# Linear attention and a softplus MLP on one core: small attention products in pairs, and an instruction planner that counts TensorE's changes of shape

## The chip, the core and the metric

The kernel runs on one core of one Trainium2 chip. The metric is the device time of the whole kernel in microseconds (us); lower is better. Times of runs are medians. The profile is one execution with the hardware profiler on; its span is close to the timed runs but not equal to them.

## What is computed

Attention without softmax, an RMS norm per head, and then an MLP with softplus:

```python
kv  = einsum('bhsd,bhse->bhde', k, v)        # batch 8, heads 8, seq 576, head_dim 64
o   = einsum('bhsd,bhde->bhse', q, kv)
x   = o / sqrt(mean(o*o, -1) + 1e-6) * g_norm
x   = x.transpose(0, 2, 1, 3).reshape(4608, 512)
out = softplus(x @ w_in) @ w_out             # w_in 512 x 2048, w_out 2048 x 512
```

All inputs are float32 in range and accuracy, and the result has to keep float32 accuracy.

## The kernel before, in words

**Exact products from three.** The large matmuls use TensorE's fp32r type. To keep float32 accuracy every operand is split into three parts (`high`, `low`, `less`, on ACT and DVE), and every product is three matmuls that are summed in PSUM.

**Attention.** For each batch `kv_of` (L625) forms k times v in five pieces of eight 64-wide matmuls (four pieces of 512 positions, one of the remaining 64), summed in one PSUM bank; the matmuls are at L654. The k and v tiles of the four main pieces come from the ring `e`, which has four slots, two for each piece; those of the fifth have slots of their own. For each of the 36 tiles of 128 tokens, `rows` (L660) turns q, multiplies it with kv in sixteen 64x64 matmuls (`out_rows`, L673), and normalizes: square on ACT, sum on DVE, the root on GpSimd, the product on DVE. The first twelve tiles are turned by TensorE (L691 for x, L729 for q); later ones are turned on DVE and go through HBM. These small products use only a part of TensorE's array at a time, unlike all other matmuls, which use all 128x128 of it. In the trace each of these float32 matmuls has two records, so that a piece of L654 is x16 and a tile of L673 is x32.

**MLP, first pass.** `step` (L798) takes a block of 384 tokens and one chunk of 128 of the 2048 hidden units: twelve matmuls of 384 columns (L812), softplus and splitting, then three groups of three matmuls of 512 columns (L819), one for each 128 tokens, summed in PSUM over the chunks of the block. Four blocks take 4 chunks and eight take 6: 64 steps. The attention work of later tokens is mixed in between.

**MLP, wide passes.** `wide_step` (L977) takes 512 tokens and a pair of chunks, with seven products (a fast scheme in the manner of Strassen) instead of eight, each of six matmuls of 256 columns (L999), with copies and sums on ACT and DVE in between (L1040, L1044, L1023, L1026, L1048), then splitting (L1056, L1059, L1062) and eight groups of three matmuls of 512 columns (L1069). There are 48 such steps in two passes. Their inputs, sums and differences of parts of x, are prepared by `units_of` (L892): loads of x and of forms that were kept (L909), a subtraction on DVE (L923), and the split (L959 on ACT, L962 and L965 on DVE). Weights of later chunks are converted from their raw form (L393 to L423), stored, loaded again (L508), combined (`both`, L512) and split. At the end of a group of steps `leave` (L857) copies the sums out of PSUM on ACT (L860) and stores them: with a plain store, or in the first wide pass with an accumulating DMA that GpSimd issues (L876). In the second wide pass partial sums are loaded and put into PSUM before (`enter`, L850, loads at L854).

**What sets the order.** No instruction is placed by hand. Every piece of work is a `Task` with an engine, a planned duration, its predecessors, the buffer slots that it takes and gives back, and a position `pos` (`add`, L76). `Plan.order` (L85) simulates the engines: for each engine it finds the tasks that could start first, looks at all that could start within `SOON` = 150 ns after that, and takes the one of lowest `pos`. The order that comes out is the order in which the instructions are issued; each engine then runs its own in that order, waiting for semaphores. Positions come from the 79 numbers in `P0` to `P3` (L232 to L236): when weights are fetched and converted, how early x and k, v and q are prepared, how the groups of a wide step lie against each other. Where TensorE would have nothing to do in the plan before the first pass is under way, the planner puts in a warm-up matmul (`warm`, L1148, recorded at L1150).

Of the kernel before, what the change touches and what calls it, by code (L numbers as in the profile page):

```python
# [55 lines left out]
class Plan:  # L56
# [18 lines left out]

    def add(self, engine, ns, run, after=(), pos=0.0, take=(), give=(), size=0, behind=None, follows=None):  # L76
# [5 lines left out]
        t.behind = behind  # L82
        return t

    def order(self):  # L85
# [30 lines left out]
        dma_free = 1500  # L116
        last_read = {}
        done, left = [], len(self.tasks)
        while left:
            best = None  # L120
            for engine, tasks in ready.items():
                options = []
                for t in tasks:
                    at = max(engine_free[engine], t.ready)
                    if t.size:
                        at = max(at, dma_free - 2500)
                    for i, s in enumerate(t.take):
                        others = sum(u.ring == s.ring for u in t.take[:i])
                        if engine == "SP" and s.ring in ("m", "n"):
                            others += self.KEEP  # L130
                        if len(free[s.ring]) <= others:
                            break
                        at = max(at, sorted(free[s.ring])[sum(u.ring == s.ring for u in t.take[:i])][0])
                    else:
                        options.append((at, t))
                if not options:
                    continue
                first = min(at for at, _ in options)
                at, t = min(((at, t) for at, t in options if at <= first + self.SOON),
                            key=lambda o: (o[1].pos, o[0]))  # L140
                if engine == "PE" and self.spare and self.spare[-1].start is None:
                    ring, run, ns, _ = self.spare
                    begin = max(engine_free["PE"], self.BEGIN, min(free[ring])[0] if free[ring] else at)
                    if begin + ns <= at:
                        s = Slot(ring)
                        at, t = begin, Task("PE", ns, lambda s=s: run(s), [], None, [s], [s], 0)
                        s.readers = 1
                if best is None or at < best[0]:
                    best = (at, t)
# [6 lines left out]
            for s in t.take:  # L156
# [27 lines left out]
def kernel(  # L184
# [24 lines left out]
    nc = tc.nc  # L209
# [21 lines left out]

    P0 = [-56.63, -20.32, -32.46, -13.58, -22.9, -4.89, -7.19, 1.72, -73.06, -41.99, -41.77, -22.79, -44.57, -21.25, -14.8, -8.6, 1.67, -29.08, 17.25, 10.29, 6.58, 8.78, -6.26, 3.54, 1.45, 13.48, -15.35, 7.9, 12.17, 8.99]  # L232
    CONVERT, FETCH, EARLY, LATER = P0[:8], P0[8:16], P0[16:27], P0[27:]
    P1 = [50.69, 53.68, 57.04, 32.49, 105.47, 132.19, 42.4, 60.71, 74.8, 108.41, 128.47, 137.43]
    P2 = [23.63, 36.5, 43.45, 50.53, 60.37, 65.43, 64.44, 117.03, 68.8, 102.64, 29.3, 15.31, 28.43, 80.7, 97.59, 71.63, 81.78, 77.98, 144.53, 143.71, 1.95]
    P3 = [3.31, 1.4, 5.36, -0.89, 1.94, 3.54, 1.55, 2.86, 2.68, -0.6, 3.76, -0.15, 0.77, -1.77, 1.87, 1.35]  # L236
    SPLIT = {p: (P1[i], P1[6 + i]) for i, p in enumerate((2, 3, 4, 5, 6, 7))}
# [379 lines left out]
    kv_ready = {}  # L617
    o_tasks = {}

    def x_pos(t):  # L620
# [4 lines left out]
    def kv_of(b):  # L625
# [4 lines left out]
        bank = slot(f"s{b}" if b < 2 else "tp")  # L630
        last = None
        MAIN = 4 * P
        for p in range(NP + 1):
# [223 lines left out]
    def leave(ph, t, bank, done, pos):  # L857
# [328 lines left out]
```

## Time and profile before

890.5 us median of 3 runs (889.25 to 891.43). The profiled execution spans 893.1 us.

| engine | busy us | share of the span |
|---|---|---|
| PE (TensorE matmul) | 870.3 | 97% |
| PEld (TensorE weight load) | 760.9 | 85% |
| DVE (VectorE) | 684.4 | 77% |
| ACT (ScalarE) | 542.6 | 61% |
| POOL (GpSimd) | 113.9 | 13% |

| group | matmuls (records) | mean ns of one record |
|---|---|---|
| L812, first pass, first product | 768 | 339 |
| L819, first pass, second product | 576 | 398 |
| L999, wide passes, first products | 2016 | 281 to 286 |
| L1069, wide passes, second product | 1152 | 393 to 396 |
| L673, q times kv | 576 (1152) | 223 |
| L654, k times v | 320 (640) | 228 to 233 |

How to read it: the durations of matmuls in the table overlap each other, because TensorE is pipelined, and their ends are modelled. What one more matmul costs is seen from start to start, in the chain of waits or the timeline. DMA moved 157.62 MB in the span, 176 GB/s on the mean.

### The profile page before, as it was taken

The numbers are of one execution on the slowest core, as the hardware profiler recorded it, in microseconds if no ns is written. First come the engines' busy times: TensorE is split into PE (matmuls) and PEld (weight loads), VectorE is DVE, ScalarE is ACT, GpSimd is POOL, SyncE is SP. The second block draws the span as 40 slices with busy tenths as digits, with TensorE's granted clock in tenths as the row PEclk, the third lists the DMA queues.
The fourth block names the chain that finished last, engine by engine and source line by source line (L and its number), as shares of the span: only waits on it lengthen the run. The fifth ranks groups of instructions, "written<-read, shape, count | busy, mean of one in ns | idle before, by whom it ended". The sixth has DMA issues, their size and how long they took to land.

```text
span 893.1 us, 16939 instructions
## 1 busy us (share of the span) xinstructions
PE 870.3 (97%) x6459; PEld 760.9 (85%) x6459; DVE 684.4 (77%) x956; ACT 542.6 (61%) x1015; POOL 113.9 (13%) x115
## 2 busy tenths in 40 slices
PE   7889999999999999999999989999999999999997
PEld 5678888888888899988888978888887988999996
DVE  6888878778688888799998778778776765667662
ACT  4776555435344466776757646556768755666764
POOL 0433321222222200001101101101101000000000
PEclk9999999999999999999999999999999999999999
DMA  9999998589883673548776648657655623566643
GB/s 252 256 239 248 244 208 240 107 183 221 221 168 123 164 226 118 181 138 208 212 201 137 162 128 240 147 153 175 141 153 106 201 90 113 177 188 182 185 130 94
DMA packets 234448, 157.62 MB, mean 176 GB/s; under 512 B 105728, under 2 KB 197888, under 8 KB 234368
## 3 DMA queue, kind: packets, MB, share of 16 engines
q1 hardware_dynamic: 229024, 147.11, 60.7%
q0 software_dynamic: 5184, 9.44, 7.4%
q8 instruction: 50, 0.82, 0.4%
q14 instruction: 30, 0.25, 0.1%
q10 hardware_dynamic: 160, 0.00, 0.0%
HBM read 103.55 MB, written 52.95 MB: 175 GB/s over the span
## 4 chain that ended last, share of the span: by engine, by line
PE 61%; issue 27%; DMA 4%; POOL 3%; DVE 3%; ACT 1%; SPq 0%; POOLq 0%; ACTq 0%; DVEq 0%
PE banks L819 15%; PE banks L812 15%; PE banks L1069 13%; PE banks L999 12%; POOL part L876 3%; PE banks L654 2%; PE banks L673 2%; DMA raw<-in_moe_w_in_dram 1%; DMA part<-m 1%; DMA loads<-in_v_dram 1%; DMA w<-in_q_dram 1%; PE banks L691 1%; DVE g_False L1062 0%; DVE gv L1059 0%; ACT m L860 0%
## 5 line engine op out<-in xcount | busy, mean ns | idle before, releaser
L1069 PE MATMUL banks<-pieces,gv 128*128 128x512 f32 x624 | 195.4, 394 | 0.2 <-ACT m L860 0.2
L812 PE MATMUL banks<-units,pieces 128*128 128x384 f32 x768 | 147.1, 339 | 0.0
L819 PE MATMUL banks<-pieces,gv 128*128 128x512 f32 x576 | 146.5, 398 | 0.0
L999 PE MATMUL banks<-units,pieces 128*128 128x256 f32 x1008 | 140.3, 282 | 0.0
L999 PEld LDWEIGHTS banks<-units,pieces 128*128 128x128 f32 x1008 | 133.6, 190 | 7.5 <-ACT g_True L1023 0.6
L812 PEld LDWEIGHTS banks<-units,pieces 128*128 128x128 f32 x768 | 134.2, 188 | 5.2 <-ACT half L834 0.3
L819 PEld LDWEIGHTS banks<-pieces,gv 128*128 128x128 f32 x576 | 105.7, 188 | 21.2
L1069 PE MATMUL banks<-pieces,g_False 128*128 128x512 f32 x312 | 122.6, 393 | 0.5 <-DVE g_False L1062 0.5
L1069 PEld LDWEIGHTS banks<-pieces,gv 128*128 128x128 f32 x624 | 108.5, 189 | 16.3 <-ACT m L860 0.4
L1059 DVE TENSOR_TENSOR gv<-g_True,gv 128x1024 fp32r<-128x1024 f32 x48 | 58.7, 1223 | 41.7 <-ACT gv L1056 41.4
L834 ACT ACTIVATE half<-banks 128x384 f32<-128x384 f32 x64 | 31.4, 490 | 86.4 <-PE banks L812 85.4
L876 POOL DMA_DIRECT2D part<-m x36 | 31.8, 960 | 329.3 <-ACT m L860 313.9
L1069 PEld LDWEIGHTS banks<-pieces,g_False 128*128 128x128 f32 x312 | 58.6, 188 | 14.8 <-DVE g_False L1062 1.5
L1026 ACT ACTIVATE g_True<-banks 128x256 f32<-128x256 f32 x96 | 36.7, 382 | 52.0 <-PE banks L999 51.1
L681 POOL TENSOR_TENSOR r<-r,half 128x8 f32<-128x8 f32 x36 | 65.8, 1827 | 3.0
L999 PE MATMUL banks<-early,pieces 128*128 128x256 f32 x432 | 61.8, 286 | 4.4 <-ACT banks L1044 3.6
L999 PEld LDWEIGHTS banks<-early,pieces 128*128 128x128 f32 x432 | 58.0, 193 | 8.3 <-ACT banks L1044 5.0
L1062 DVE SCALAR_TENSOR_TENSOR g_False<-gv 128x1024 fp32r<-128x1024 f32 x48 | 58.8, 1225 | 1.5
L962 DVE TENSOR_TENSOR units<-loads,units 128x1024 fp32r<-128x1024 f32 x39 | 47.6, 1221 | 15.3 <-ACT units L959 13.5
L1048 DVE TENSOR_TENSOR g_True<-banks,g_True 128x512 f32<-128x512 f32 x48 | 33.1, 689 | 33.6 <-ACT g_True L1023 20.2
L823 DVE TENSOR_TENSOR gv<-half,gv 128x384 fp32r<-128x384 f32 x64 | 35.3, 552 | 29.4 <-ACT gv L836 28.8
L860 ACT ACTIVATE m<-banks 128x512 f32<-128x512 f32 x72 | 41.8, 595 | 18.0 <-PE banks L1069 10.8
(117 smaller groups left out, 1408.1 us busy)
## 6 DMA issues: line engine op xcount, KB each, us to landing
loads<-x SPq DMA_DIRECT2D x180, 128.0 KB, 2.7
loads<-form SPq DMA_DIRECT2D x45, 256.0 KB, 3.0
part<-m SPq DMA_DIRECT2D x36, 256.0 KB, 3.1
form<-loads SPq DMA_DIRECT2D x36, 256.0 KB, 3.1
part<-m POOLq DMA_DIRECT2D x36, 256.0 KB, 5.6
m<-part SPq DMA_DIRECT2D x36, 256.0 KB, 3.1
raw<-in_moe_w_in_dram SPq DMA_DIRECT2D x16, 512.0 KB, 5.2
loads<-in_k_dram SPq DMA_DIRECT2D x32, 256.0 KB, 4.9
```

What stands on the lines that cost most here:

```text
L681: nc.gpsimd.tensor_tensor(out=r.tile, in0=r.tile, in1=half, op=ALU.pow)
L812: nc.tensor.matmul(hp, lhsT=w_in.tile[:, i, kd * P:(kd + 1) * P], rhs=xv.tile[:, i, kd], start=(m == 0), stop=(m == 3 * KD - 1))
L819: nc.tensor.matmul(mine[i].tile, lhsT=gv.tile[:, m, i * P:(i + 1) * P], rhs=w_out.tile[:, m], start=(c == cs[0] and m == 0), stop=(c == cs ...
L823: nc.vector.tensor_tensor(out=gv.tile[:, 1], in0=g.tile, in1=gv.tile.bitcast(F32)[:, 0], op=ALU.subtract)
L860: a = add("ACT", 690 if ph == LAST else 600, lambda: nc.scalar.activation(new(ot, [P, d_model]), bank.tile, func=AF.Copy, scale=scale if p ...
L876: part[t] = dst, add("POOL", 1200, lambda: nc.gpsimd.dma_start(out=dst, in_=ot.tile, accum_op=ALU.add), [a, st], pos, [], [ot], 900)
L962: nc.vector.tensor_tensor(out=part_of(1, F32R), in0=xl.tile if m > 1 else xl.tile[:, 0], in1=part_of(0), op=ALU.subtract)
L999: nc.tensor.matmul(place(q), lhsT=w[:, m, at:at + P], rhs=dst.tile[:, m, v, kd] if u < 6 else dst.tile[:, m, kd], start=(u == 0 and not m ...
L1026: nc.scalar.activation(dst, src, func=AF.Softplus, scale=1.0 + E)
L1059: nc.vector.tensor_tensor(out=gvt(1, F32R), in0=gt(), in1=gvt(0), op=ALU.subtract)
L1062: nc.vector.scalar_tensor_tensor(out=gt(F32R), in0=gvt(1), scalar=-RADIX, in1=gvt(0), op0=ALU.mult, op1=ALU.add)
L1069: nc.tensor.matmul(mine[i].tile, lhsT=(gvt(m, F32R) if m < 2 else gt(F32R))[:, c, i * P:(i + 1) * P], rhs=outs[c].tile[:, m], start=fresh ...
```

## The change

The small products of attention are planned so that they stand together, and the planner is told what a change of shape costs.

- Every TensorE task has a kind: `kv` for a piece of k times v, `rows` for a tile of q times kv, `all` for the rest. The planner adds a price (`SWITCH`) where the kind changes, and the durations of the small tasks are lowered (600 to 470, 640 to 484 ns), since the price is now apart.
- Among the tasks that it could take, it stays with the kind it is in, if that is a small one.
- For batches 2 to 7 the pieces of k times v are tied together as first and second, third, fourth and fifth: the later ones of a group follow the first at once (`follows`), and the first waits for the loads of all. For tiles from the thirteenth on, the second tile of each block of three is tied to the first in the same way.
- The planned cost of the accumulating store in the first wide pass is changed.
- All the positions in `P0` to `P3` are chosen anew.

No arithmetic, tile, buffer or DMA is added or removed.

```diff
+    SWITCH = {("all", "rows"): 90, ("all", "kv"): 90, ("rows", "all"): 250, ("kv", "all"): 250, ("rows", "kv"): 140, ("kv", "rows"): 140}
+    TOGETHER, PATIENCE = 1, 0.0
...
-                at, t = min(((at, t) for at, t in options if at <= first + self.SOON),
-                            key=lambda o: (o[1].pos, o[0]))
+                options = [(at, t) for at, t in options if at <= first + self.SOON]
+                small = [o for o in options if engine == "PE" and o[1].kind != "all"]
+                if small:
+                    rest = [o for o in options if o[1].kind == "all"]
+                    if kind != "all":
+                        options = [o for o in small if o[1].kind == kind] or small
+                    elif rest and len(small) < self.TOGETHER and (
+                            min(o[1].pos for o in small) + self.PATIENCE > min(o[1].pos for o in rest)):
+                        options = rest
+                at, t = min(options, key=lambda o: (o[1].pos, o[0]))
...
+            if t.engine == "PE":
+                t.ns += self.SWITCH.get((kind, t.kind), 0)
+                kind = t.kind
             t.start = at
...
-    P3 = [3.31, 1.4, 5.36, -0.89, 1.94, 3.54, 1.55, 2.86, 2.68, -0.6, 3.76, -0.15, 0.77, -1.77, 1.87, 1.35]
+    P3 = [2.14, 1.08, 5.88, -0.92, 1.63, 2.67, 2.6, 1.59, 2.29, 2.01, 3.35, 0.34, -0.08, -0.89, 3.05, -0.96]
...
-            last = add("PE", 600, run, lds + [last], pos + 0.5 * p, [bank] if p == 0 else [], [ks, vs])
+            if b >= 2 and (p % 2 or tail):
+                first.after.extend(lds)
+            last = add("PE", 470, run, lds + ([last] if b < 2 else []), pos + 0.5 * p, [bank] if p == 0 else [], [ks, vs], kind="kv",
+                       follows=last if b >= 2 else None)
+            if p % 2 == 0 and not tail:
+                first = last
...
-        a = o_task = add("PE", 640, out_rows, turned + need, pos, [o], [qT])
+        second = t >= BY_PE and t % TB == 1
+        if second:
+            rows_done[t - 1].after.extend(turned + need)
+        a = o_task = add("PE", 484, out_rows, turned + need, pos - second, [o], [qT], kind="rows", follows=rows_done.get(t - 1))
+        rows_done[t] = a
...
-            part[t] = dst, add("POOL", 1200, lambda: nc.gpsimd.dma_start(out=dst, in_=ot.tile, accum_op=ALU.add),
-                               [a, st], pos, [], [ot], 900)
+            part[t] = dst, add("POOL", 1000, lambda: nc.gpsimd.dma_start(out=dst, in_=ot.tile, accum_op=ALU.add),
+                               [a, st], pos, [], [ot], 1900)
```

`P0`, `P1` and `P2` change in the same way as `P3`, in all their numbers.

More of the change, by code (lines that the diff above doesn't have):

```diff
@@ L74, in slot, with add @@
         return Slot(ring)
-    def add(self, engine, ns, run, after=(), pos=0.0, take=(), give=(), size=0, behind=None, follows=None):
+    def add(self, engine, ns, run, after=(), pos=0.0, take=(), give=(), size=0, behind=None, follows=None, kind="all"):
         t = Task(engine, ns, run, [a for a in after if a is not None], pos, list(take), list(give), size)
@@ L82, in add @@
         t.behind = behind
+        t.kind = kind
         return t
@@ L117, in order @@
         last_read = {}
+        kind = "all"
         done, left = [], len(self.tasks)
@@ L146, in order @@
                         at, t = begin, Task("PE", ns, lambda s=s: run(s), [], None, [s], [s], 0)
+                        t.kind = "all"
                         s.readers = 1
@@ L230 @@
     LAST = 2
-    P0 = [-56.63, -20.32, -32.46, -13.58, -22.9, -4.89, -7.19, 1.72, -73.06, -41.99, -41.77, -22.79, -44.57, -21.25, -14.8, -8.6, 1.67, -29.08, 17.25, 10.29, 6.58, 8.78, -6.26, 3.54, 1.45, 13.48, -15.35, 7.9, 12.17, 8.99]
+    P0 = [-49.84, -17.88, -35.99, -11.25, -19.79, -5.76, -6.59, 2.32, -72.59, -44.84, -44.11, -27.86, -36.42, -23.37, -11.42, -1.64, 8.39, -28.07, 13.62, 9.21, 8.15, 12.69, -9.98, 5.3, 1.39, 25.83, -11.96, 7.88, 13.2, 7.36]
     CONVERT, FETCH, EARLY, LATER = P0[:8], P0[8:16], P0[16:27], P0[27:]
-    P1 = [50.69, 53.68, 57.04, 32.49, 105.47, 132.19, 42.4, 60.71, 74.8, 108.41, 128.47, 137.43]
-    P2 = [23.63, 36.5, 43.45, 50.53, 60.37, 65.43, 64.44, 117.03, 68.8, 102.64, 29.3, 15.31, 28.43, 80.7, 97.59, 71.63, 81.78, 77.98, 144.53, 143.71, 1.95]
-    P3 = [3.31, 1.4, 5.36, -0.89, 1.94, 3.54, 1.55, 2.86, 2.68, -0.6, 3.76, -0.15, 0.77, -1.77, 1.87, 1.35]
+    P1 = [50.98, 57.72, 60.23, 40.06, 110.11, 134.41, 41.79, 46.64, 73.31, 91.73, 127.74, 138.75]
+    P2 = [23.23, 37.56, 36.87, 47.12, 56.32, 61.0, 53.55, 123.6, 69.05, 107.19, 42.49, 16.95, 48.29, 68.01, 98.48, 79.47, 86.8, 80.78, 146.51, 128.13, -4.65]
+    P3 = [2.14, 1.08, 5.88, -0.92, 1.63, 2.67, 2.6, 1.59, 2.29, 2.01, 3.35, 0.34, -0.08, -0.89, 3.05, -0.96]
     SPLIT = {p: (P1[i], P1[6 + i]) for i, p in enumerate((2, 3, 4, 5, 6, 7))}
@@ L618 @@
     o_tasks = {}
+    rows_done = {}
     def x_pos(t):
@@ L630, in kv_of @@
         bank = slot(f"s{b}" if b < 2 else "tp")
-        last = None
+        last = first = None
         MAIN = 4 * P
```

## The prediction

> **What bounds the kernel now.** I read the page first, then the busy time by stretches, the chain of waits in one stretch, and the timeline around TensorE's longest stop. On the page:
>
> ```profile
> PE 870.3 (97%) x6459; PEld 760.9 (85%) x6459; DVE 684.4 (77%) x956; ACT 542.6 (61%) x1015; POOL 113.9 (13%) x115
> ...
> PE   7889999999999999999999989999999999999997
> DMA  9999998589883673548776648657655623566643
> ...
> q1 hardware_dynamic: 229024, 147.11, 60.7%
> q0 software_dynamic: 5184, 9.44, 7.4%
> ```
>
> TensorE (PE) sets the time nearly everywhere; only in the first slices is it below nine tenths, and there the DMA engines are full. Busy time by stretches (columns: stretch, its length, then PE, PEld, DVE, ACT and POOL busy, clock, DMA share, GB/s) says the same:
>
> ```profile
> 0.00:99.00 99.00, 87.72 (x1046) 68.82 (x1047) 78.50 (x136) 62.86 (x121) 29.40 (x33) 0.97 1.01 246
> 99.00:310.00 211.00, 211.00 (x1952) 182.37 (x1951) 167.57 (x285) 100.16 (x196) 50.60 (x45) 1.00 0.80 188
> ```
>
> From 99 to 310 us, where most attention work is mixed with the MLP's first pass, PE never stops. But busy is not the same as useful. The chain of waits inside that stretch (start, us, what) is one unbroken PE line, and it shows what a small product costs (L673 is one token tile's q times kv, L654 one piece of k times v, L812 and L819 the large MLP products):
>
> ```profile
> 144.34 2.11 PE banks L812 x12
> 146.45 2.10 PE banks L819 x9
> 148.55 0.62 PE banks L673 x32
> 149.18 2.31 PE banks L812 x12
> 151.49 0.62 PE banks L654 x16
> 152.10 2.26 PE banks L819 x9
> 154.36 0.62 PE banks L654 x16
> 154.98 0.62 PE banks L673 x32
> 155.60 2.30 PE banks L812 x12
> ...
> 191.11 0.70 PE banks L819 x3
> 191.81 1.09 PE banks L673 x64
> 192.90 1.59 PE banks L819 x6
> ```
>
> A lone L673 takes 0.62 us and the next twelve L812 take 2.31 instead of 2.11: 0.82 together. Two L673 in a row take 1.09, so a second one costs 0.47. The change of shape out and back is therefore 0.62 + 0.20 - 0.47 = 0.35 us, whether the trip holds one group or two. Between L654 and L673 (154.36 to 155.60) each still takes 0.62: a change among the small shapes costs 0.15.
>
> **What the Trainium skill says.** "TensorEngine Tiling (Array Packing)", section Key Properties, says that changing the tiling mode drains TensorE, unlike changing only the tile. It gives no price; the trace agrees, with the 0.35 and 0.15 us above. "Perfetto Trace Analysis", section Tensor Engine Instruction, says that ACT, DVE and GpSimd are strictly first in, first out, and that PE reorders only weight loads. The trace of the wide passes agrees: one late DMA stops everything behind it on three engines (shown below).
>
> **The change part by part.** *Pairs and shape-counting.* The multiplications are the same (320 L654, 576 L673, 768 L812, 576 L819, 2016 L999, 1152 L1069); only warm-up matmuls go from 47 to 45. What moves is the order. I counted trips out of the full shape in both instruction orders, split at the ninth L812 group (99 us in the trace of before):
> - late part: 34 trips and 7 changes among small shapes before, 16 and 8 after. Before: 34 x 0.35 + 7 x 0.15 = 12.95 us; after: 16 x 0.35 + 8 x 0.15 = 6.80 us. Saved: 6.15 us, all on PE's unbroken line, so on the path.
> - early part: 24 and 5 before, 23 and 1 after: 9.15 against 8.20, 0.95 us saved. I count it as nothing, because DMA hides it (share 1.01, 246 GB/s up to 99 us), and because pairing adds a wait there. The k and v loads live in four slots, two pieces' worth, so pieces 3 and 4 of a batch load only once 1 and 2 are multiplied. In the trace the load released by a piece at 59 us was issued at 60.10 and landed 6.69 us later; its consumer started at 66.93, after 0.93 us idle. Both loads now follow one pair, so the last lands some 8 us after it. By the durations above, the new order puts 5.5 us of PE work between the pairs of batch 2, 7.3 for batch 3, and 9 to 16 for batches 4 to 7. So 2 to 3 us of waiting at batch 2, 1 at batch 3, none later. Queued behind such a wait on PE are turns of q and x and MLP groups, and ACT and DVE wait for those. Some of it falls in time that DMA had to have anyway. I take 0 net for the early part, with +1 (gain) and -3 (loss) as ends.
>
> *Batches 4 to 7 earlier.* Their k-v products begin after 87, 118, 169 and 214 us of PE work instead of 92, 132, 181 and 222, with the same megabytes queued ahead (24.6, 33.2, 42.7, 49.4 against 24.9, 33.2, 43.0, 49.4). Before, the first load of batch 4 was issued at 97.25 and its product started at 110.95, some 8 us after landing, so 5 us less is still enough. For batch 5, 14 us less is about all there is. The DMA share of 0.80 in this stretch leaves room. I take 0, with 3 us lost as the bad end.
>
> *The planner's other numbers.* POOL's accumulating store is now planned at 1000 ns issue and 1900 DMA instead of 1200 and 900. The lines above bear the second out: 7.4% of 893.1 us over 36 stores is 1.84 us of all engines for each, while the plain queue moves the same 0.262 MB in 60.7% x 893.1 x 0.262 / 147.11 = 0.97 us. No instruction changes.
>
> *Positions in the wide passes (367 us on).* The 79 position numbers differ, so order differs there too. Mixing L999 with L1069 more finely, as the new order does, costs PE nothing: a group of six L999 took 0.71 us before either kind, and one L1069 0.23. PE's work there is 2016 x 0.118 + 1152 x 0.230 = 503 us plus some 3 of others; it ran from 366.98 to about 885.7, or 518.7. So about 13 us are stops. The largest:
>
> ```profile
> 513.71 0.68 ACT L393 ACTIVATE sq<-raw 128x512 bf16<-128x512 bf16 x1 [2.01 <-DMA raw<-in_moe_w_out_dram]
> 516.19 0.39 PE L1069 MATMUL banks<-pieces,g_False 128*128 128x512 f32 x1
> 516.74 0.69 DVE L923 TENSOR_TENSOR loads<-loads 128x512 f32<-128x512 f32 x1 [2.60 <-DMA loads<-x]
> 517.47 1.06 ACT L959 ACTIVATE units<-loads 128x1024 fp32r<-128x1024 f32 x1 [3.08 <-DVE loads L923]
> 519.79 0.37 ACT L1044 COPY banks<-banks 128x256 f32<-128x256 f32 x1
> 520.21 2.71 PE L999 MATMUL banks<-early,pieces 128*128 128x256 f32 x12 [3.63 <-ACT banks L1044]
> ```
>
> A load of x is late, DVE waits for it, ACT's split waits for DVE, and the copy that PE needs stands behind the split: 3.8 us, and 1.6 more while the next 24 matmuls run slow (4.47 us against 24 x 0.118 = 2.83). Then 2.4 us around 402 (L965, L1040) and 2.1 at 680, where DVE stood at a weight load landing beside POOL's accumulating stores. In the new order splits come somewhat later against the steps they feed: counted on DVE in finished steps, a lead of 0.50 instead of 0.72 on average, later in 17 of 72 groups and earlier in 2. That gives loads more time before they block ACT and DVE, and products less after. Sums are drained two and two instead of four at a time. With accumulating stores planned at their real cost, a collision like 516 should be rarer. I take 2 us of the 13 as gone; ends: 8 us gone, and 11 more, two further stops like that at 516.
>
> Sum: -6.15 - 0 - 0 - 2 = -8.15: 890.5 - 8.15 = 882.4 us.
>
> **The rivals.**
> - *More falls away* (0.16): early gain real (0.95) and 8 of the 13 us of stops gone: 890.5 - 6.15 - 0.95 - 8 = 875.4. For it: the stops are accidents of order, and the planner's DMA price is now right. Against: the old order was planned too and has 13 us of them.
> - *Loads become the wait* (0.17): batches 2, 3 and 5 stand for 3 + 3 us and the wide passes are as before: 890.5 - 6.15 + 3 = 887.4 if half is absorbed by slack already lost at the start. For it: DMA full to 111 us. Against: share 0.80 after that.
> - *The other side: slower* (0.14): the later splits bring two more stops like 516: 890.5 - 6.15 + 11 = 895.4. For it: a lead of half a step on DVE is little, and the queues are strict. Against: moving only 17 of 72 groups.
>
> **How the numbers follow.** The likeliest (0.53) is 882.4. Low end 874.0, just beyond the rich rival; high end 891.0, which takes in the load rival and leaves out most of the slow one. Faster than 887.8: the likeliest, the rich rival and about half of the load rival, 0.79; within 0.3% (887.8 to 893.2): the rest of that and a little of the slow one, 0.10; slower: 0.11.
>
> **What would show it.** Right: from the ninth L812 group to the end of that pass, lone small groups become few, two L673 in a row take about 1.1 us and a pair L654 about 1.1, PE stays unbroken, and the stretch is some 6 us shorter for the same groups. Early: PE idle on loads of k and v at batches 2 and 3. Wide passes: PE's stops sum to about 11 us. Wrong if lone groups cost less than 0.35 once elsewhere, if PE idles on loads between 100 and 150 us, or if the stops in the wide passes differ from 13 us by more than the 6 us saved; the last is the largest unknown.

## The result and the profile after

882.16 us median of 4 runs (880.35 to 884.47) against 890.5 us (889.25 to 891.43): a ratio of 0.9909, 95% interval 0.9882 to 0.9935. The forecast was 882.4 us. The total is right; how it comes about is right in part only. Two of its terms were off by 3 us and more, in opposite directions, and that they cancel is luck.

In the new listing the lines of the prediction are L671 (k times v, was L654), L695 (q times kv, was L673), L838 and L845 (first pass, were L812 and L819), L1025 and L1095 (wide passes, were L999 and L1069), L409 (the square of a raw weight on ACT, was L393) and L398 (the fetch of that raw weight). The page after:

```profile
PE 861.5 (98%) x6457; PEld 758.8 (86%) x6457; DVE 682.9 (77%) x956; ACT 538.7 (61%) x1015; POOL 111.8 (13%) x115
...
PE   7899999999999999999999998999999999999998
...
q1 hardware_dynamic: 229024, 147.11, 61.3%
q0 software_dynamic: 5184, 9.44, 7.0%
```

Same work, same bytes, and TensorE (PE) is still the bound; it is busy 8.8 us less. The same two stretches by busy time (length, then PE, PEld, DVE, ACT, POOL, clock, DMA share, GB/s):

```profile
0.00:99.00 99.00, 88.30 (x1036) 70.09 (x1040) 78.86 (x137) 61.88 (x121) 27.72 (x31) 0.97 0.99 245
99.00:310.00 211.00, 208.96 (x1994) 184.97 (x1988) 176.15 (x302) 105.16 (x207) 51.73 (x48) 1.00 0.82 196
```

From 99 to 310 us PE held 211.00 us without a gap before. Now it has 2.04 us of gaps, and still does more: the matmuls that start in the stretch are worth 201.4 us at the plain pace that is defined below, against 198.3. Both belong to the change. The chain of waits in that stretch shows the first (start, us, what):

```profile
175.93 2.10 PE banks L845 x9
178.03 2.10 PE banks L838 x12
180.12 2.09 PE banks L845 x9
182.21 1.09 PE banks L695 x64
183.30 2.29 PE banks L838 x12
185.59 2.10 PE banks L845 x9
187.69 2.10 PE banks L838 x12
189.79 0.67 PE banks L695 x32
```

Lone small groups have become few. A pair of tiles takes 1.09 us and the next twelve L838 2.29 instead of 2.10. The pair's own work is 2 x 0.47, so the trip costs 1.09 - 0.94 + 0.19 = 0.34 us: the predicted price, paid once for two tiles. The timeline shows the second thing (start, us, engine, line, operation, tiles; in brackets the idle time before it and what ended it):

```profile
137.09 0.69 PE L671 MATMUL banks<-loads 128*64 128x64 f32 x16
138.98 0.69 PE L671 MATMUL banks<-loads 128*64 128x64 f32 x16 [1.21 <-DMA loads<-in_v_dram]
```

This is batch 5, pieces one and two. The piece that should follow at once waits 1.21 us for its v, whose load had been issued at 131.79. The prediction took such waits as 0, with 3 us as the bad end.

To compare orders I use one measure throughout, the time **over the plain pace**: every group of PE is taken from its start to the start of the next, and from that are subtracted the matmuls in it at the pace of an unbroken stretch (2.10/12 = 0.175 us for one of L838, 2.09/9 = 0.232 of L845, 0.118 of L1025, 0.230 of L1095, 0.235 of a warm-up, 0.47 for a tile of L695 or a piece of L671). What remains is changes of shape, waits, and matmuls that ran slow. The groups that turn x, q and weights are left out, with any wait that stands directly behind one. "Early" ends at the ninth L838 group, "late" at the last matmul of the first pass.

| over the plain pace, us | before | after |
|---|---|---|
| early | 22.31 | 21.51 |
| late | 13.07 | 10.14 |
| of it priced: trips and changes among small shapes | 12.95 (34 and 7) | 6.80 (16 and 8) |
| of it stops | 0.1 | 3.3 |
| wide passes | 14.70 | 9.69 |

That is 0.8 + 2.9 + 5.0 = 8.7 us; two warm-ups less (0.5) and shorter turns (0.7) bring it to the 10.0 us by which the last matmul starts earlier in the trace (888.34 to 878.37). The medians differ by 8.3 us only, since the execution profiled before took 894.86 us, 4.4 over its median, and that after 884.47, 2.3 over. Of 103 further timed runs of the kernel before, three took as long as the profiled one, so its stop at 516 us need not be in the usual execution. These shares are those of two executions; the other profiles below show which of them hold.

One part of the two largest stops is not waiting. The prediction saw the 24 matmuls after the stop at 516 run slow; the stretches of 3.4 us after that stop and after the one at 530 us of the changed kernel say why (before, then after):

```profile
520.50:523.90 3.40, 3.40 (x18) 3.40 (x18) 3.37 (x4) 0.65 (x3) 0.00 (x0) 0.50 0.59 155
534.70:538.10 3.40, 3.40 (x15) 3.11 (x14) 2.21 (x4) 0.82 (x3) 0.86 (x1) 0.50 0.64 100
```

The granted clock is 0.50 there, and 1.00 in the stretches that follow, so about 1.7 us of each stop comes after the wait has ended.

### The profile page after: what moved, and what is told of

The parts are those of the page before. It is cut to its first block, busy times and chain, and to the rows that moved or that the text cites. A ratio compares the mean times of both kernels' runs of the same rounds, so it can differ in the third digit from the quotient of the medians.

```text
span 882.7 us, 16941 instructions
## 1 busy us (share of the span) xinstructions
PE 861.5 (98%) x6457; PEld 758.8 (86%) x6457; DVE 682.9 (77%) x956; ACT 538.7 (61%) x1015; POOL 111.8 (13%) x115
## 4 chain that ended last, share of the span: by engine, by line
PE 88%; DMA 5%; DVE 3%; ACT 2%; issue 1%; POOL 1%; SPq 0%; DVEq 0%; ACTq 0%
PE banks L1095 30%; PE banks L1025 27%; PE banks L838 14%; PE banks L845 13%; PE banks L695 2%; DMA g<-in_moe_w_out_dram 2%; PE banks L671 2%; DMA raw<-in_moe_w_in_dram 1%; DMA raw<-in_moe_w_out_dram 1%; DMA early<-in_q_dram 1%; PE banks L713 1%; DMA loads<-in_v_dram 1%; POOL r L703 0%; PE banks L751 0%; DVE half L707 0%
## 5 line engine op out<-in xcount | busy, mean ns | idle before, releaser
L1095 PE MATMUL banks<-pieces,gv 128*128 128x512 f32 x624 | 196.0, 395 | 0.0
L1025 PEld LDWEIGHTS banks<-units,pieces 128*128 128x128 f32 x1140 | 151.5, 191 | 16.5 <-ACT banks L1070 6.2
L1025 PE MATMUL banks<-units,pieces 128*128 128x256 f32 x1140 | 158.3, 284 | 4.4 <-ACT banks L1070 3.1
L845 PE MATMUL banks<-pieces,gv 128*128 128x512 f32 x576 | 147.3, 397 | 0.2 <-DVE gv L853 0.2
L838 PE MATMUL banks<-units,pieces 128*128 128x384 f32 x768 | 145.9, 338 | 0.0
L838 PEld LDWEIGHTS banks<-units,pieces 128*128 128x128 f32 x768 | 134.7, 188 | 5.0
L845 PEld LDWEIGHTS banks<-pieces,gv 128*128 128x128 f32 x576 | 105.8, 188 | 21.0 <-DVE gv L853 0.5
L1095 PE MATMUL banks<-pieces,g_False 128*128 128x512 f32 x312 | 122.7, 393 | 0.1
L1095 PEld LDWEIGHTS banks<-pieces,gv 128*128 128x128 f32 x624 | 105.6, 190 | 11.8
L1095 PEld LDWEIGHTS banks<-pieces,g_False 128*128 128x128 f32 x312 | 58.7, 188 | 13.9 <-ACT banks L1066 0.5
L985 ACT ACTIVATE units<-loads 128x1024 fp32r<-128x1024 f32 x42 | 44.5, 1059 | 21.3 <-PE banks L1025 17.5
L988 DVE TENSOR_TENSOR units<-loads,units 128x1024 fp32r<-128x1024 f32 x42 | 51.3, 1221 | 5.5 <-ACT units L985 5.3
L991 DVE SCALAR_TENSOR_TENSOR units<-units 128x1024 fp32r<-128x1024 f32 x42 | 51.3, 1222 | 1.4
L1082 ACT ACTIVATE gv<-g_True 128x1024 fp32r<-128x1024 f32 x48 | 50.9, 1060 | 1.0
```

What stands on the lines that cost most here:

```text
L838: nc.tensor.matmul(hp, lhsT=w_in.tile[:, i, kd * P:(kd + 1) * P], rhs=xv.tile[:, i, kd], start=(m == 0), stop=(m == 3 * KD - 1))
L845: nc.tensor.matmul(mine[i].tile, lhsT=gv.tile[:, m, i * P:(i + 1) * P], rhs=w_out.tile[:, m], start=(c == cs[0] and m == 0), stop=(c == cs ...
L985: nc.scalar.activation(part_of(0, F32R), xl.tile if m > 1 else xl.tile[:, 0], func=AF.Copy, scale=DOWN)
L988: nc.vector.tensor_tensor(out=part_of(1, F32R), in0=xl.tile if m > 1 else xl.tile[:, 0], in1=part_of(0), op=ALU.subtract)
L991: nc.vector.scalar_tensor_tensor(out=part_of(2, F32R), in0=part_of(1), scalar=-RADIX, in1=part_of(0), op0=ALU.mult, op1=ALU.add)
L1025: nc.tensor.matmul(place(q), lhsT=w[:, m, at:at + P], rhs=dst.tile[:, m, v, kd] if u < 6 else dst.tile[:, m, kd], start=(u == 0 and not m ...
```

## Experiments

Theory: the price of trips (from the full shape to a small one and back) makes the gain, and the rest is stops that the order makes. Rivals: the new positions, or the right cost of the accumulating store, make it. All ratios are to the kernel before, run on the same chip.

| run | time, us | ratio [95%] | late: all, priced, stops | wide |
|---|---|---|---|---|
| pairs only | 885.3 | 0.9945 [0.9925, 0.9965] | 11.80, 6.80, 5.0 | 10.81 |
| positions only | 904.33 | 1.0152 [1.0131, 1.0173] | 21.07, 13.05, 8.0 | 6.87 |
| store cost undone | 885.46 | 0.9952 [0.9936, 0.9969] | 11.94, 6.80, 5.1 | 6.58 |
| two transfers moved | 892.21 | 1.0033 [1.0022, 1.0044] | 14.62, 6.80, 7.8 | 10.45 |
| the change again | 883.41 | 0.9934 [0.9913, 0.9954] | 11.51, 6.80, 4.7 | 9.93 |
| pieces of k times v untied | 890.93 | 1.0014 [1.0001, 1.0027] | 12.99, 9.05, 3.9 | 7.60 |
| positions shaken | 891.79 | 1.0022 [1.0007, 1.0036] | 17.04, 7.00, 10.0 | 7.29 |
| one conversion moved | 882.46 | 0.9913 [0.9895, 0.9932] | 11.76, 6.80, 5.0 | 4.68 |
| later positions new, no pairs | 903.02 | 1.0143 [1.0126, 1.0160] | 26.95, 12.40, 14.6 | 9.55 |
| later positions old, with pairs | 896.55 | 1.0065 [1.0047, 1.0082] | 12.39, 6.80, 5.6 | 17.83 |
| store cost only | 890.69 | 1.0004 [0.9994, 1.0014] | 13.09, 12.95, 0.1 | 10.43 |

### Pairs alone

The changed kernel with `P0` to `P3` and the store's planned cost of before:

```diff
-    P3 = [2.14, 1.08, 5.88, -0.92, 1.63, 2.67, 2.6, 1.59, 2.29, 2.01, 3.35, 0.34, -0.08, -0.89, 3.05, -0.96]
+    P3 = [3.31, 1.4, 5.36, -0.89, 1.94, 3.54, 1.55, 2.86, 2.68, -0.6, 3.76, -0.15, 0.77, -1.77, 1.87, 1.35]
...
-            part[t] = dst, add("POOL", 1000, ...
-                               [a, st], pos, [], [ot], 1900)
+            part[t] = dst, add("POOL", 1200, ...
+                               [a, st], pos, [], [ot], 900)
```

> The pairs and the shape-counting planner of the changed kernel, with the positions and the accumulating store's planned cost of the kernel before. Late part of the attention: 16 trips out of the full shape and 8 changes among small shapes, as in the changed kernel. Theory (each trip costs 0.35 us, each small change 0.15, wherever it stands): the late part's time over the plain matmul pace falls from 13.1 us to 6.8 plus what it stops, the wide passes keep about 14 us of stops, 884.3 us in all (882 to 887). Rival (the new positions bring the gain, pairs alone only turn changes of shape into waits): 889 us or more.

885.3 us, inside the range of the theory. The trips fall to 16 and 8 and the price with them, but 5.0 us of stops come in the late part, 2.8 of them idle on loads of v (0.93 us at 107, 1.19 at 109, 0.67 at 215). So in the late part the rival is mostly right: of 6.15 us saved, 5.0 turn into stops. By the ratios (0.9945 against 0.9909 and 0.9934 for the whole change) pairs alone are worth half of the gain or more; where the rest of it comes from in this run is not shown.

### Positions alone

The other half: all new numbers and the new store cost, but no ties, no price and no staying with a small kind.

```diff
-                small = [o for o in options if engine == "PE" and o[1].kind != "all"]
+                small = []
...
-                t.ns += self.SWITCH.get((kind, t.kind), 0)
+                t.ns += 0
...
-            if b >= 2 and (p % 2 or tail):
+            if False:
...
-        second = t >= BY_PE and t % TB == 1
+        second = False
```

(The old durations of 600 and 640 ns are back, and no `follows` is given.)

> The positions and the accumulating store's planned cost of the changed kernel, with the ties, the price of a change of shape and the lower planned durations of the small products taken out, so that the planner is that of the kernel before. Late part: 36 trips and 3 small changes. Theory: the late part again costs 36 x 0.35 + 3 x 0.15 = 13.1 us over the plain pace, the wide passes stop about 9.7 us as in the changed kernel, 885.5 us in all (884 to 889). Rival (positions were only good together with the pairs): stops of other kinds appear and it is 890 us or more.

904.33 us: the theory fell. The positions taken alone cost 15 us. The trips stay (36), 8.0 us of stops come to the late part (2.52 us idle on a v load at 156.30, 1.50 on DVE at 373.40), and early, where PE waits 1.51 us for ACT at 109.56, the sum is 27.67. Yet the wide passes, with 6.87, are better than in either kernel. The new numbers suit the planner that they were chosen with, not the old one.

### The store's planned cost

First taken out of the changed kernel, then put into the kernel before, by itself:

```diff
-            part[t] = dst, add("POOL", 1000, ...
-                               [a, st], pos, [], [ot], 1900)
+            part[t] = dst, add("POOL", 1200, ...
+                               [a, st], pos, [], [ot], 900)
```

> The changed kernel with the accumulating store planned at its old cost (1200 ns issue, 900 ns of DMA); trips as in the changed kernel. Theory A (the right planned cost is what thins out the stops in the wide passes): stops there go back to about 14 us and the time to 886 to 887. Theory B (the stops are accidents of order, whatever the planned cost): stops anywhere between 7 and 15 us, with no tie to the stores; 880 to 887.

> The kernel before with only the accumulating store's planned cost of the changed kernel. Late part: 34 trips and 7 small changes, 13.0 us by the price and measured. Theory (stops in the wide passes are accidents of order, whatever the planned cost): attention as before, wide passes 7 to 15 us of stops, 884 to 891. Rival (the right cost thins them out): wide passes under 10 us and the time 884 to 886.

Without it the wide passes stop less (6.58), not more, so the right cost isn't why they gained. What the kernel loses against the changed one, if anything (the intervals overlap), it loses to other stops on loads, at 75, 144 and 252 us. In the kernel before it changes nothing that can be measured (1.0004). But the profile of that run has no stop like the one at 516 us of before. Its busy time from 500 to 540 us, and after it that of before:

```profile
500.00:540.00 40.00, 39.10 (x237) 34.04 (x237) 36.91 (x45) 23.99 (x46) 5.27 (x6) 1.00 0.70 186
```

```profile
500.00:540.00 40.00, 36.37 (x213) 32.22 (x212) 31.24 (x38) 21.09 (x38) 3.50 (x4) 0.96 0.63 168
```

Its span is 889.0 us against 893.1, while the medians are equal. The orders of the two differ in the wide passes, so this does not show that the stop at 516 is absent from most executions of before; it does show that a stop seen in one profile is not yet a term of the median. The profiled execution of this run took 890.81 us, its median is 890.69, and its first pass costs what that of the kernel before costs (13.09 and 13.07).

### The same kernel again, for its stops

> The changed kernel once more, beside the runs below. If the stops come from the order of instructions, they return in the same places with about the same length (1.4 us at batch 5, 1.4 us at 370, about 4.7 us at 530) and the time is 882 us (880.5 to 884). If they are accidents of one execution, they move or vanish.

No edit. By its ratio it gains 0.66%, where the first measurement had 0.91%; the intervals overlap. The stops come back in the same places (141 to 143, 197, 377 and 539 us), two to five us later; the one at batch 5 is now 0.60 and 1.62 us of idle time. The largest, in the first profile of the changed kernel:

```profile
530.70 0.40 PE L1095 MATMUL banks<-pieces,g_False 128*128 128x512 f32 x1
...
533.26 0.66 ACT L409 ACTIVATE sq<-raw 128x512 bf16<-128x512 bf16 x1 [4.53 <-DMA raw<-in_moe_w_out_dram]
...
533.83 0.36 ACT L1070 COPY banks<-banks 128x256 f32<-128x256 f32 x1
...
534.24 1.10 PE L1025 MATMUL banks<-units,pieces 128*128 128x256 f32 x5 [3.15 <-ACT banks L1070]
```

A raw weight of 0.5 MB, issued at 525.72 behind eight loads of x, is used at 533.26. ACT comes to its square (L409) 4.53 us too early and stands; the copy L1070, for which PE waits, is next in the queue. It is of the kind of the stop at 516 of the kernel before, with another transfer at its head.

The run with a tail of matmuls (last experiment) gives a third execution: up to the tail, TensorE's matmuls and the DMA issues stand in the same order. The waits for v at batch 5 (2.12 us at 141.42) and those at 195 and 376 return in it. The stop at 530 does not:

```profile
533.91 0.67 ACT L409 ACTIVATE sq<-raw 128x512 bf16<-128x512 bf16 x1 [1.64 <-DMA raw<-in_moe_w_out_dram]
...
534.90 0.98 PE L1025 MATMUL banks<-units,pieces 128*128 128x256 f32 x6 [0.27 <-ACT banks L1070]
```

There the wide passes come to 5.2 us over the plain pace instead of 9.7 and 9.9, and the late part to 12.3. So the stops on loads in the first pass belong to the order; the one at 530 comes in two executions of three, and both took longer than their kernel's median (884.47 and 889.49 us, 2.3 and 6.1 over it).

### Two transfers moved

Two stops were attacked in the finished order: the raw fetch ahead of batch 5's loads was put behind them, and the conversion whose square stands at 533, with the raw fetch after it, was put 5 us later.

```diff
-    for t in plan.order():
+    done = plan.order()
...
+    moved = conversion[fetches[28].tag[1]] + [fetches[29]]
+    delay = 5000
+    done = sorted(done, key=lambda t: t.start + (delay if t in moved else 0))
+    t = fetches[10]
+    done.remove(t)
+    done.insert(max(i for i, u in enumerate(done) if getattr(u, "tag", None) == ("kv", 5, 1)) + 1, t)
...
+    for t in done:
```

> The changed kernel's own order with two moves after planning: the raw weight fetch that is queued just ahead of batch 5's first k and v loads goes behind them, and one raw weight's conversion (the square that stood before the copy TensorE waited for at 534 us, with the rest of its conversion and the next raw fetch) goes 5 us of planned time later. Theory (these two stops are single late transfers ahead of strict queues): the stop of 1.4 us at batch 5 and the one of 3.3 with 1.4 of slow matmuls after it go, 877 us (875.5 to 879). Rival (DMA is short there, and the wait goes on to the next reader): 881 to 883.

892.21 us. The waits went on to the next readers, as the rival had it, but the time lies 9 us beyond even its range. The timeline of this kernel (L412 is the square, L852 is L845 of the changed kernel):

```profile
140.41 0.69 PE L678 MATMUL banks<-loads 128*64 128x64 f32 x16 [0.83 <-DMA loads<-in_v_dram]
141.75 0.67 ACT L412 ACTIVATE sq<-g 128x512 bf16<-128x512 bf16 x1 [6.51 <-DMA g<-in_moe_w_out_dram]
...
143.35 0.52 ACT L869 ACTIVATE gv<-half 128x384 fp32r<-128x384 f32 x1
...
143.93 0.80 PE L852 MATMUL banks<-pieces,gv 128*128 128x512 f32 x1 [2.83 <-ACT gv L869]
...
555.28 0.68 ACT L412 ACTIVATE sq<-raw 128x512 bf16<-128x512 bf16 x1 [3.95 <-DMA raw<-in_moe_w_in_dram]
```

PE now waits 0.83 us for the v load (1.21, and 2.22 in two pieces, in the two profiles of the changed kernel), but the fetch that made room is late for its own reader: ACT stands 6.51 us, and PE loses 2.83, then 0.89, on what stood behind; from 142.2 to 149.0 us the granted clock is 0.50 besides. In the wide pass the stop at 530 is gone and one of 3.76 us has come before 557.43: the moved fetch met its conversion, which I had not moved.

### One conversion moved

So once more, with the fetches left alone and the one conversion 3.5 us later (`moved = conversion[fetches[28].tag[1]]`, `delay = 3500`).

> The changed kernel's own order with one raw weight's conversion alone moved, by 3.5 us of planned time, so that its square stands behind the two ACT copies that it stood ahead of; no fetch is moved. Theory (the stop at 530 us is ACT and DVE standing at a raw fetch that has not landed, ahead of a copy that TensorE needs): the stop of 3.3 us and the slow matmuls after it go, no new one over 1 us comes near, wide passes 5 to 6 us of stops, 879 us (877 to 881) where the changed kernel took 882 to 883. Rival (as with the two moves together, the wait goes to the next reader): 882 to 885.

In the profile it works. From 530 to 540 us PE is busy without a gap, first in this kernel, then in the changed one:

```profile
530.00:540.00 10.00, 10.00 (x62) 8.85 (x61) 7.47 (x10) 5.44 (x11) 2.59 (x3) 1.00 1.04 263
```

```profile
530.00:540.00 10.00, 6.85 (x31) 5.74 (x30) 5.12 (x9) 3.14 (x7) 0.86 (x1) 0.83 0.82 189
```

The square starts at 536.55 without a wait, and the wide passes are down to 4.68. But the time, 882.46, is that of the changed kernel (882.16 and 883.41). It falls in the rival's range, though the wait went to no next reader. Why the 3 us do not show in the medians is not settled. It fits that the stop is not in every execution of the changed kernel, as the run with the tail shows: then the median had little of it to lose. Against the second profile of the changed kernel, which has the stop and starts its ninth L838 group at the same 100.0 us, this one is 5.0 us shorter (spans of 882.7 and 887.7 us).

### Are the ties of k times v to blame for the late stops?

```diff
-            if b >= 2 and (p % 2 or tail):
+            if False:
...
-            last = add("PE", 470, run, lds + ([last] if b < 2 else []), pos + 0.5 * p, [bank] if p == 0 else [], [ks, vs], kind="kv",
-                       follows=last if b >= 2 else None)
+            last = add("PE", 470, run, lds + [last], pos + 0.5 * p, [bank] if p == 0 else [], [ks, vs], kind="kv",
+                       follows=None)
```

> The changed kernel with the ties between pieces of k times v taken out (each piece only follows the one before, as before the change); prices, ties of the q tiles and positions stay, and the planner orders anew. Late part: 19 trips and 16 small changes, 19 x 0.35 + 16 x 0.15 = 9.05 us by the price, against 6.80. Theory (the tie makes TensorE reach the second piece before its load has landed): stops on loads of k and v in the late part are under 1 us in sum, the late part costs 9 to 10.5 us, and the time is 880 to 886. Rival (DMA is short there whatever the ties): 2 us or more of such stops stay.

890.93 us. The trips are 19 with 16 changes among small shapes (9.05 us), and 3.9 us of stops remain, 1.2 of them idle on v loads (0.75 at 149 us, 0.46 at 253). That lies between the two expectations (under 1 us, and 2 or more) and is what the changed kernel has in its first profile (1.21), so the tie is not shown to be what makes those loads late. Early it is worse than all others but positions alone (25.84 over the plain pace; idle on v loads 1.25 and 1.31 us). I had expected less lost in the late part and a better time; untying loses the whole gain.

### Positions shaken

The 79 numbers were moved at random, each by up to 0.3; those of `P3` lie between -1 and 6, those of `P0` to `P2` between -73 and 147. The start of `P3`:

```diff
-    P3 = [2.14, 1.08, 5.88, -0.92, 1.63,
+    P3 = [2.24, 1.0, 5.84, -0.91, 1.8,
```

> The changed kernel with each of its 79 positions moved by a random amount of up to 0.3 of a step. Late part: 17 trips and 7 small changes, 7.0 us by the price, so the pairs stay. Theory (what is left beside the price is accident of order that the choice of positions has kept small): late part 10 to 15 us with its stops, wide passes 7 to 15, time 884 to 892. Rival (any positions near these do as well): 880 to 884.

891.79 us. The trips stay few (17 and 7, 7.0 us), but the late stops grow to 10.0. The largest:

```profile
143.12 0.69 PE L695 MATMUL banks<-early,w 64*64 64x64 f32 x32 [0.47 <-ACT early L679]
146.93 1.14 PE L695 MATMUL banks<-early,w 64*64 64x64 f32 x32 [3.11 <-DVE w L726]
```

The turn of q on DVE (L726) came late, and from 145.3 to 152.1 us the granted clock is 0.50, so an estimated 2.6 of the 10.0 us (half of the 5.2 us that were left of that stretch when PE went on) is again slow matmuls. In this one draw the saving in trips outlives the shaking, and the freedom from stops does not.

### Later positions exchanged

`P1` to `P3` and the store cost of the new kernel in the kernel before (no pairs), and those of before in the new kernel (with pairs); `P0` stays with its planner.

> The kernel before with the positions of the weights and the wide passes (P1, P2, P3) and the accumulating store's cost of the changed kernel; the positions of attention (P0) and the planner stay as before. Late part: 32 trips and 8 small changes, 32 x 0.35 + 8 x 0.15 = 12.4 us by the price. Theory (the wide passes' part of the gain comes from their own positions): late part 12 to 14 us, wide passes 6.5 to 10, 885.5 us (883 to 888). Rival (it was an accident of the old order that anything may undo or keep): wide passes anywhere between 7 and 15 us, time 883 to 893.

> The changed kernel with P1, P2, P3 and the accumulating store's cost of the kernel before; pairs, planner and P0 stay. Late part: 16 trips and 8 small changes, 6.8 us by the price. Theory (attention's part of the gain comes from pairs with P0, the wide part from P1 to P3): late part 9 to 11 us, wide passes 11 to 15, 887 us (885 to 889). Rival (no such split, orders are luck): late part over 11 us, or wide passes under 10.

903.02 and 896.55 us: both mixtures are slower than either whole. The first has one stop that explains most of it:

```profile
174.21 0.69 PE L673 MATMUL banks<-early,w 64*64 64x64 f32 x32
...
180.32 0.67 ACT L393 ACTIVATE sq<-g 128x512 bf16<-128x512 bf16 x1 [4.47 <-DMA g<-in_moe_w_out_dram]
...
185.26 1.13 PE L673 MATMUL banks<-early,w 64*64 64x64 f32 x32 [10.36 <-DVE half L685]
```

Again a raw weight at the head: ACT and DVE wait for it, the conversion runs, and the normalization (L685) behind it on DVE lets PE go after 10.36 us. The second has most of its loss in the wide passes (17.83). There the profiles sort themselves by the numbers. With old `P1` to `P3` the four sums are 14.70, 10.43, 10.81 and 17.83 (mean 13.4). With new ones, whatever else differs, they are 9.69, 9.93, 6.87, 6.58, 7.60, 7.29 and 9.55 (mean 8.2; the runs with moved transfers left out). The two sets do not overlap, but they come close (10.43 and 9.93), and single stops of 4 to 5 us, which need not come in every execution, are a large part of the spread. Like against like the difference stays: with the large stop 14.70 before and 9.69 after, without it 10.43 (store cost only) and 5.2 (the changed kernel in the run with the tail). So some 5 us is what these profiles give for the new positions there.

### The price by itself

A tail of TensorE work alone was added after the kernel's end, so its whole time, 1201 us, is not to be compared. Groups of small matmuls stand between groups of full 128x384 ones (L1187), once in single and once in double size:

```diff
+    for like, x, n in ((rows_like, ident, 4), (kv_like, ident, 4), (square_like, ident, 4), (half_like, ident_r, 4), (square_like, ident_r, 4)):
+        for _ in range(16):
+            like(n, x)
+            full(6)
+        for _ in range(8):
+            like(2 * n, x)
+            full(12)
...
```

> The changed kernel with a tail of TensorE work behind its end, for its trace alone: small groups, each followed by six 384-column fp32r matmuls (16 times), then two small groups together followed by twelve (8 times); the difference is eight trips saved. Small groups of sixteen 64x64 float32, of eight 128x64 float32, of four whole-array 128x128 float32, of four 64-row fp32r and of four 128x128 fp32r matmuls; last, both kinds of small products in a row. If the price is that of the array's shape: 0.35 us a trip for the first two, much the same for 64-row fp32r, and about 0 for both 128x128 kinds. If it is that of the number type: 0.35 for all three float32 kinds and 0 for both fp32r kinds. A change among small shapes: 0.15 us.

Two single trips and one double one do the same work; what they differ by is the price of a trip. The timeline of PE (64x64 matmuls are L1192, whole-array 128x128 ones L1208; most lines of the full groups between them are left out):

```profile
906.38 0.69 PE L1192 MATMUL banks<-ident_r 64*64 64x64 f32 x32
907.00 1.32 PE L1187 MATMUL banks<-ident_r 128*128 128x384 f32 x6
908.25 0.69 PE L1192 MATMUL banks<-ident_r 64*64 64x64 f32 x32
...
915.38 1.16 PE L1192 MATMUL banks<-ident_r 64*64 64x64 f32 x64
918.76 1.16 PE L1192 MATMUL banks<-ident_r 64*64 64x64 f32 x64
...
1022.70 1.05 PE L1208 MATMUL banks<-ident_r 128*128 128x128 f32 x8
1024.63 1.05 PE L1208 MATMUL banks<-ident_r 128*128 128x128 f32 x8
...
1030.43 1.95 PE L1208 MATMUL banks<-ident_r 128*128 128x128 f32 x16
1034.30 1.95 PE L1208 MATMUL banks<-ident_r 128*128 128x128 f32 x16
```

64x64: two single trips take 2 x (908.25 - 906.38) = 3.74 us, a double one 918.76 - 915.38 = 3.38; 0.36 us for a trip. Whole array: 2 x (1024.63 - 1022.70) = 3.86 against 1034.30 - 1030.43 = 3.87; nothing. In the same way 128x64 float32 costs 0.35, and 64-row matmuls in fp32r, the type of the large products, 0.35. A row of both small shapes, 128x64 then 64x64, leaves about 0.16 us for the change between them.

## Why the prediction was right, and where not

**The bound and the price: right.** PE sets the time throughout. The 0.35 us that were read from three lines of one chain stand up to all 34 trips of the late part of before (12.95 us priced, 13.07 found) and to the tail by itself (0.36 and 0.35; about 0.16 among small shapes). It is the price of the array's shape, as the Trainium skill has it ("TensorEngine Tiling (Array Packing)", section Key Properties: changing the tiling mode drains TensorE), and not of the number type: the tail has the price with fp32r matmuls of 64 rows and not with whole-array float32 ones. Counting trips in the two instruction orders gave the right 6.15 us.

**"Batches 4 to 7 earlier ... I take 0": mis-sized.** Of the 6.15 us, the late part gave back 3.3 in stops that before did not have, and kept 2.9. In the three other executions with this order of TensorE (the change again, one conversion moved, the run with the tail) it gave back 4.7, 5.0 and 5.5 and kept 0.8 to 1.6; there the wait at batch 5 is followed by 3.4 us at the clock of 0.50. So the term is beyond even its bad end, "3 us lost", and batch 5, where "14 us less is about all there is", has the largest of the stops (1.4 us in the first profile). The sign given for it, PE idle on loads between 100 and 150 us, came. All runs with the pairs have between 3.3 and 10.0 us of late stops, whatever the positions; so have those with the new positions and no pairs (8.0 and 14.6), and only the order of the kernel before has none. Neither moving the fetch ahead nor untying the pieces took the loads' waits away, so the cause is shown no further than this: the load was issued at 131.79, PE was ready for it at 137.77 (138.98 less 1.21), and it took 7.2 us to come.

**Early part, 0 net: not decided.** The waits that I had feared at batch 2 did not come in the profile after. Its pairs, and then its third and fourth pieces in the profile of "one conversion moved", where TensorE's order is the same:

```profile
62.62 1.15 PE L671 MATMUL banks<-loads 128*64 128x64 f32 x32
...
69.46 1.15 PE L671 MATMUL banks<-loads 128*64 128x64 f32 x32
```

```profile
71.33 0.69 PE L678 MATMUL banks<-loads 128*64 128x64 f32 x16
73.70 0.69 PE L678 MATMUL banks<-loads 128*64 128x64 f32 x16 [1.69 <-DMA loads<-in_v_dram]
```

In the first there is no idle time before either pair; in the second the fourth piece waits 1.69 us for its v, which is what the prediction had feared there. The ninth L838 group starts at 96.60 us in the profile after, but at 98.12, 99.99 and 100.01 in the three others with this order, and at 99.09 before. The difference is below what executions of one order differ by here.

**The store's cost, no effect by itself: right** (1.0004). Its use as a reason, "a collision like 516 should be rarer", is not borne out: in the profile of the changed kernel without it the wide passes stop less (6.58 against 9.69).

**"I take 2 us of the 13 as gone": too small.** The 13 were too few to begin with: the prediction let the wide passes end at about 885.7 us, but their last matmul starts at 888.34, and the measure used here finds 14.70. They were also read from one execution that took 4.4 us more than the median. The two traces give 5.0 gone, and like against like, with and without the large stop, it is 5.0 and 5.2, within the range of 8 gone to 11 more. That the later splits do it was argued from the order and has not been tried apart.

So the sum came out right because the late part kept 3 to 5 us less than the forecast, the wide passes gave some 3 us more, and the early part, taken as 0, may have given a little. That is luck: nothing in the prediction makes the two errors cancel. The rivals in their pure forms fell: no more than this fell away (875.4), loads became a wait but a smaller one (887.4), and the wide passes did not get worse (895.4). The last was no idle fear: with the same pairs, other positions gave 885.3, 891.8 and 896.6 us.

## What to carry to other kernels

Where TensorE never stops, take the price of a change from start to start in its unbroken chain, count the changes in both instruction orders, and multiply; here the late part of the kernel before agreed within 1% over 34 trips. Then look for what the new order makes late: a transfer whose reader stands ahead of TensorE's supplier in a strict queue (ACT, DVE) costs PE a good part of that reader's wait (3.15 of 4.53 us, 3.72 of 6.51), and in the one try here, moving the transfers moved the wait to their next readers. Before a stop is attacked, a second profile of the same kernel tells whether it is there each time: the stop at 530 was in two executions of three. When a planner's rules change, its tuned positions go with them; half of such a change says little about the whole, since here one half alone was 1.5% slower.

## What the runs showed of the hardware that was not expected

- In these five forms the price of a trip goes with the shape of the array and not with the number type: 0.36 us for 64x64 and 0.35 for 128x64 in float32 and 0.35 for 64 rows in fp32r, but 0.00 for whole-array float32 among fp32r matmuls (0.01 for whole-array fp32r).
- After its long waits here, TensorE ran at a lower clock for a while. In the fourteen profiles, PE stands idle for 2.12 us or more ten times after the first 100 us, and each time the granted clock is 0.50 for at least 3.4 us about its restart. Waits of 2.06 and 1.84 us had no such stretch; waits of 1.19, 1.29 and 1.62 us had one, the first and the last of these shortly behind another wait. What decides it is not shown.
- One instruction stream does not start alike each time. While DMA is full, the fifth L838 group of the changed kernel began at 63.70 us in one execution and at 67.11 in another; from its ninth group to the last matmul the two took 782.0 and 783.6 us. Two more executions with this order began their ninth group at 98.12 and 100.01 us.
